# A channel-attention kernel: 160 rows packed in place of 144, 23 plain rows stored first, and a scale in two halves

## The chip, the cores and the metric

The kernel runs on one core of one Trainium2 chip. The metric is the device time of one execution in microseconds (us). The time before is 729.73 us, the median of three executions (729.52 to 731.41). A profile is one further execution, recorded by the hardware profiler; the profile before is of an execution of 729.56 us, whose instructions and transfers span 727.8 us.

The core's engines are named as in the profile: PE (TensorE: matmuls; PEld is its weight load), DVE (VectorE), ACT (ScalarE), POOL (GpSimd) and SP (SyncE). Loads from HBM are issued on SP's queue, stores on ACT's; both use the same 16 DMA engines.

## The reference

```python
H = W = C = 384;  r = 96                 # x: [1, 384, 384, 384] bf16, w1: [384, 96], w2: [96, 384]
xf  = x.reshape(B, H * W, C)
gap = jnp.mean(xf, 1)
gmp = jnp.amax(xf, 1)
h_a = relu(gap @ w1)
h_m = relu(gmp @ w1)
scale = sigmoid(h_a @ w2 + h_m @ w2)
return x * scale[:, None, None, :]
```

The whole of x (147,456 positions of 384 channels, 113.25 MB) has to be read before the first output can be computed, since the scale depends on the mean and the maximum over all positions. Then x is multiplied by one number per channel and written. What of x was kept on the chip after the first reading need not be read again.

## The kernel before

**Rows.** The positions are spread over the 128 partitions, 1152 on each. One position on all partitions is called a row here: 384 bf16 values on each partition, 98,304 bytes in all. A block of n rows is one transfer of n x 768 contiguous bytes for each partition.

**First pass.** All 1152 rows are loaded in the order of the list `loads`, by one DMA for each entry. Three large tiles, `slots` (44 rows each, `x` in the profile), are filled in turn; FILLS gives for each of 25 fills the rows that will be packed (always 16, `PAIR`) and the rows that are only looked at. For every load PE adds the rows up by matmuls with ones (`sums`, L274: three matmuls for up to four rows), and DVE takes the maximum into the 11 rows of `acc` (`larger`, L311). Consecutive maxima go alternately into two parts of `acc` (PARTS). Towards the end `acc` is folded from 11 rows to 6 and from 6 to 3 (FOLDS: how many loads before the end, and to what width), after which the parts are smaller.

**What stays on the chip.** Of the 1152 rows, 337 are kept on the chip between the passes: 132 that the three slots hold at the end of the first pass (`stay_b`, STAYING gives the pieces in which they are loaded), 35 in the plain rows of the tile `room` (`room_b`, ROOM_PIECES), 10 in `late`, 16 in PSUM (`kept_ps`) and 144 in packed form. The other 815 are read a second time: the 11 rows with which `acc` began, between the passes (`refill`), and 804 in the second pass (AGAIN: 18 blocks of 44 and one of 12).

**Packing.** Sixteen rows at a time, two groups of 8 (PACKED). ACT copies the high bytes apart (L321), takes signs (L324), copies the low bytes into the room (L339), PE mixes the high bytes with weights (L334, 18 matmuls in three groups of six), ACT writes the mixed code (L344) and tests that the code can be undone (L341 and L346, into the scratch tile `test`). 8 rows become 6 rows' worth of bytes (PLANE_ROWS) in `room`, whose layout is ROOM_ROWS plain rows and then the packed planes. While packing goes on, the plain rows are scratch space (`high`, `sign`, `test`, `diag`, flags); only after the last pack and after `judge` (L353 to L355, one number that says if all packs were good; if not, a branch at the end stores the packed rows again from x) can they be loaded.

**Between the passes.** `turn_sums` and `tail_sums` bring the sums of the last rows (SUM_TAIL: how many loads are summed by the second of them) and of all others into one column for each 128 channels, w1 and w2 are loaded, and the hidden layer of the mean is computed on PE and ACT. DVE folds `acc` to one row, PE transposes it (L418), DVE reduces (L419), PE multiplies by w1 (L422), DVE adds the hidden layers (L423), PE multiplies by w2 for all partitions (L424), ACT takes the sigmoid into `scale_bc` (L425).

**Second pass.** `order` lists the tiles that hold rows, in the order in which they are multiplied and stored. `put` multiplies a piece in place on DVE (L430) and issues its store on ACT's queue (L446). The order before is slot 0, slot 1, the room (ROOM_TURN = 2), slot 2, and then the blocks of AGAIN in the slots. FIRST_STORES and FIRST_READS give the pieces of the first tiles. The 11 rows of `acc` are stored after three pieces (ACC_STORES_AT). After LEAD tiles the loads of the next blocks into the free slots are issued on SP; each waits until the store of what the slot held has landed. From the turn after UNPACK_FROM on, each turn unpacks one group of 8 rows into the room (`unpack`: ACT L464, DVE L467 and L470, and the multiplication L430). The groups' places in the room (`packed_place`) are 8 rows apart; a group may only be unpacked where no plane lies that is still needed. The first four groups are stored as soon as they are there (`early_b`), which frees their 32 rows for the last four groups; the rest goes out in three stores near the end (ROOM_STORES), behind them the late rows, the last block and the rows from PSUM.

SP, ACT and DVE run in the program's order (`manual_schedule` in the second pass), and a wait of one instruction holds up all that stand behind it on the same engine. PE's order is laid down at build time.

Of the kernel before, what the change touches and what calls it, by code (L numbers as in the profile page):

```python
# [8 lines left out]
ACT = mybir.ActivationFunctionType  # L9
ALU = mybir.AluOpType  # L10
# [15 lines left out]

PACKED = 8
GROUP = 4
N_PACK = 18
PAIR = 2 * PACKED  # L30
HIGH = 0x3800
HIGH_BITS = 0x8700
PLANE_ROWS = PACKED // 2 + PACKED // GROUP
# [7 lines left out]

ROOM_ROWS = 35
EARLY = 4
assert all(
    ROOM_ROWS + (PLANE_ROWS * k) >= (k + 1) * PACKED for k in range(N_PACK - EARLY)
) and ROOM_ROWS + PLANE_ROWS * (N_PACK - EARLY) >= EARLY * PACKED

ACC_ROWS = 11  # L50
PARTS = {11: ((0, 6), (6, 11)), 6: ((0, 3), (3, 6)), 3: ((0, 3),)}
LATE_ROWS = 10
# [2 lines left out]

PSUM_PIECES = (4, 12)
FILLS = (
    ((16,), ()), ((), (40,)), ((), (44,)), ((16,), (28,)), ((), (44,)), ((), (44,)),
    ((16,), (28,)), ((), (43,)), ((), (27,)), ((16,), (27,)), ((), (44,)), ((), (44,)),
    ((16,), (28,)), ((), (36,)), ((), (40,)), ((16,), (20,)), ((), (36,)), ((), (32,)),  # L60
    ((16,), (28,)), ((), (27,)), ((), (28,)), ((16,), (24,)), ((), (23, 21)), ((), (20,)),
    ((16,), (12, 16)),
)
ROOM_PIECES = (8, 6, 5, 6, 5, 5)
STAYING = ((16, 14, 14), (11, 11, 11, 6, 5), (4, 4, 3, 3, 6, 6, 3, 3, 6, 3, 3))
ROOM_LOADS = 2
LATE_AT = (1, 3)
LATE_PIECES = (10,)

FOLDS = {9: 6, 1: 3}  # L70

AGAIN = (44,) * 18 + (12,)
FIRST_STORES = ((4, 4, 4, 7, 8, 8, 9), (10, 11, 11, 12), (16, 19))
FIRST_READS = ((10, 11, 11, 12), (44,))
LEAD = 2
ROOM_TURN = 2
ACC_STORES_AT = 3
ACC_STORES = ((6, 11), (0, 6))
UNPACK_FROM = 4
ROOM_STORES = (44, 36, 32)  # L80
SUM_TAIL = 3
MM_ROWS = 4


# [1 line left out]
def kernel(  # L86
# [7 lines left out]
    nc = tc.nc  # L94
    P = nc.NUM_PARTITIONS
    B_, H, W, C = x.shape
    R = w1.shape[1]
# [27 lines left out]
    early_b = block_of(EARLY * PACKED)  # L125
    packed_b = block_of(n_packed - EARLY * PACKED)
    late_b = block_of(LATE_ROWS)
    room_b = block_of(ROOM_ROWS)
# [10 lines left out]
    hid = small[0:R, 8:9]  # L139
# [14 lines left out]
    scale_bc = consts.tile([P, C], BF16)  # L154
    w2_sb = scale_bc[0:R, :]
# [11 lines left out]
    n_grp = PACKED // GROUP  # L167
# [15 lines left out]
    acc = hole[:, 0:A, :]  # L183
    late = hole[:, A:A + LATE_ROWS, :]

    scratch = PAIR + 2 * n_grp + PAIR // 2
    high = room[:, 0:PAIR, :]
    sign = room[:, PAIR:PAIR + 2 * n_grp, :]
    test = room[:, PAIR + 2 * n_grp:scratch, :]
    diag = room[:, scratch:scratch + 2, :].rearrange("p n c -> p (n c)").rearrange("p (k m) -> p k m", m=P)  # L190
    flags_bf = room[:, scratch + 2, 0:N_PACK // 2]
    scrap = room[FLAG:FLAG + 1, scratch + 2, N_PACK:N_PACK + N_PACK // 2]
# [20 lines left out]

    def packed_place(k):

        if k < EARLY:
            return early_b, k * PACKED
        if k < N_PACK - EARLY:
            return packed_b, k * PACKED
        return packed_b, (k - N_PACK + EARLY) * PACKED  # L220


    first = (-1 - len(FILLS)) % NS
# [5 lines left out]
    done, k = A, 0  # L229
# [15 lines left out]
    def pieces_of(block, pieces, buf):  # L245
        j = 0
        for m in pieces:
            loads.append((block, j, j + m, buf, j, ()))
            j += m
        assert j == block[1]  # L250

    for s, pieces in enumerate(STAYING):
        if s == ROOM_LOADS:
            pieces_of(room_b, ROOM_PIECES, room)
        n = len(loads)
        pieces_of(stay_b[s], pieces, slots[s])
        if s == LATE_AT[0]:
            j = 0
            for i, m in enumerate(LATE_PIECES):
                loads.insert(n + LATE_AT[1] + i, (late_b, j, j + m, late, j, ()))  # L260
                j += m
            assert j == LATE_ROWS
    n_loads = len(loads)
    judged_at = max(i for i, load in enumerate(loads) if load[5]) + 2
    tail_rows = sum(hi - lo for _, lo, hi, *_ in loads[n_loads - SUM_TAIL:])
# [100 lines left out]
    for i, (block, lo, hi, buf, at, groups) in enumerate(loads):  # L366
# [24 lines left out]
        j = 0  # L391
# [29 lines left out]
    for q in range(CQ):  # L421
        nc.tensor.matmul(hTm_ps, lhsT=w1_sb[:, q, :], rhs=gT[:, q, 1:2], start=(q == 0), stop=(q == CQ - 1))  # L422
    nc.vector.scalar_tensor_tensor(out=hid, in0=hTm_ps, scalar=0.0, in1=hid_a, op0=ALU.max, op1=ALU.add)  # L423
    nc.tensor.matmul(z_ps, lhsT=hid.to_broadcast([R, P]), rhs=w2_sb, start=True, stop=True)  # L424
    nc.scalar.activation(out=scale_bc, in_=z_ps, func=ACT.Sigmoid)  # L425


    def multiply(dst, src):
        n = dst.shape[1]
        nc.vector.tensor_tensor(  # L430
            out=dst, in0=src, in1=scale_bc.unsqueeze(1).to_broadcast([P, n, C]), op=ALU.mult
        )

    def put_acc():
# [4 lines left out]
    def put(block, buf, pieces, acc_at=None):  # L439
        j = 0  # L440
        for i, m in enumerate(pieces):
            if i == acc_at:
                put_acc()
            rows = buf[:, j:j + m, :]
            multiply(rows, rows)
            nc.scalar.dma_start(out=part(orr, block, j, j + m), in_=rows)  # L446
            j += m
        assert j == block[1]
# [7 lines left out]

    def unpack(k):
        low, code = planes(k)
        j = packed_place(k)[1]
        rows = room[:, j:j + PACKED, :]  # L460
        words = rows.bitcast(U16)
        bits = acc[:, 0:PACKED, :].bitcast(U16)
        more = acc[:, PACKED:PACKED + n_grp, :].bitcast(U16)
        nc.scalar.activation(out=words, in_=low, func=ACT.Copy, bias=float(HIGH))  # L464

        def field(out, shift, op, mask):
            nc.vector.tensor_scalar(out=out, in0=code, scalar1=shift, scalar2=mask, op0=op, op1=ALU.bitwise_and)  # L467

        def add(out, a, b):
            nc.vector.tensor_tensor(out=out, in0=a, in1=b, op=ALU.bitwise_or)  # L470

        for r in range(GROUP - 1):
            field(bits[:, r * n_grp:(r + 1) * n_grp, :], 4 * r, ALU.logical_shift_left, HIGH_BITS)
        last = bits[:, PACKED - n_grp:PACKED, :]
        field(more, 12, ALU.logical_shift_left, 0x8000)
        field(last, 4, ALU.logical_shift_right, 0x0700)
        add(last, last, more)
        add(words, words, bits)
        multiply(rows, rows)
# [10 lines left out]
        get(block, slots[s], reads.pop(0) if reads else (block[1],))  # L490
        order.append((block, s))

    room_left, j = [], EARLY * PACKED
    for m in ROOM_STORES:
        room_left.append((j, j + m))
        j = (j + m) % packed_b[1]
    assert j == EARLY * PACKED

    def put_room(count):
        for _ in range(count):  # L500
# [7 lines left out]
    while k < len(order):  # L508
        block, s = order[k]
        buf = room if s is None else slots[s]  # L510
        put(block, buf, stores.pop(0) if stores else (block[1],), None if k else ACC_STORES_AT)
        k += 1
        if k == LEAD:
            for j in range(k):
                read_into(order[j][1])
        elif k > LEAD:
            read_into(s)
        if k > UNPACK_FROM and unpacked < N_PACK:
            unpack(unpacked)
            unpacked += 1  # L520
            if unpacked == EARLY:
                nc.scalar.dma_start(out=part(orr, early_b, 0, early_b[1]), in_=room[:, 0:early_b[1], :])
        if k == n_turns - 2:
            put_room(1)
        elif k == n_turns - 1:
            put_room(2)
            multiply(late, late)
            nc.scalar.dma_start(out=part(orr, late_b, 0, LATE_ROWS), in_=late)
# [48 lines left out]
```

## Time and profile before

| what | value |
|---|---|
| median of three executions | 729.73 us |
| the profiled execution: time, span | 729.56 us, 727.8 us |
| DVE busy | 556.4 us, 76% of the span |
| ACT busy | 250.3 us, 34% |
| PE busy | 156.4 us, 21% |
| SP's queue (loads): share of the 16 DMA engines | 62.6%, 193.52 MB |
| ACT's queue (stores) | 36.4%, 113.25 MB |

"Busy" is the time in which an engine executed an instruction. An instruction's release is inferred from semaphore events. The profile's page also cuts the span into 40 slices of 18.2 us and gives, for each, the busy tenths of each engine, the granted PE clock, the share of the DMA engines' time and the bytes moved. The same can be asked for any stretch of time; the columns are then the stretch, its length, the busy time and count of PE, PEld, DVE, ACT and POOL, the granted PE clock (1.00 is full), the DMA share (which can pass 1 a little) and GB/s. The chain of waits follows the work that ended last back to its start.

### The profile page before, as it was taken

The page shows a single profiled execution, that of the slowest core. Times are in us where ns is not written, and L with a number is a line of the kernel's source. Part 1 is how long each engine was busy: PE and PEld are TensorE (multiplying, and loading weights), DVE is VectorE, ACT ScalarE, POOL GpSimd, SP SyncE. Part 2 cuts the span into 40 slices and gives each one's busy share as a digit, 9 for nine tenths or more (in the row PEclk, how much of TensorE's full clock was granted, in tenths as well). Part 3 has the DMA queues.
Part 4 walks back from the last instruction along what each step waited for, and adds up shares of the span by engine and source line. Part 5 has one row for each costly group of instructions (what it writes and reads, how often), then busy time and mean ns, then how long its engine had stood idle before and what let it go on. Part 6 is the DMA issues. An engine that isn't in the chain of part 4 may idle for free.

```text
span 727.8 us, 3125 instructions
## 1 busy us (share of the span) xinstructions
PE 156.4 (21%) x1069; PEld 50.5 (7%) x1078; DVE 556.4 (76%) x422; ACT 250.3 (34%) x135; POOL 0.7 (0%) x6
## 2 busy tenths in 40 slices
PE   3656654555666460000000000000000000000000
PEld 1211211111121120000000000000000000000000
DVE  6689999999999998978177677277767766666920
ACT  4994985978998400002011111011111011111100
POOL 0000000000000000000000000000000000000000
PEclk9975788877876755555555555555555555555555
DMA  9999999999999989999999999999999999999997
GB/s 384 426 440 413 429 444 420 426 435 419 429 425 421 416 315 355 404 430 449 423 446 416 438 445 420 446 416 446 436 425 442 419 444 420 444 440 431 435 421 340
DMA packets 19248, 306.96 MB, mean 422 GB/s; under 512 B 2496, under 2 KB 2848, under 8 KB 7200
## 3 DMA queue, kind: packets, MB, share of 16 engines
q1 hardware_dynamic: 13328, 193.52, 62.6%
q10 hardware_dynamic: 5904, 113.25, 36.4%
q8 instruction: 8, 0.13, 0.1%
q14 instruction: 8, 0.07, 0.0%
HBM read 193.51 MB, written 113.25 MB: 421 GB/s over the span
## 4 chain that ended last, share of the span: by engine, by line
DMA 60%; DVE 18%; ACT 14%; issue 2%; PE 1%; SPq 0%; DVEq 0%; ACTq 0%
DMA x<-in_x_dram 39%; DMA out_dram<-x 21%; DVE x L430 12%; ACT room L321 6%; ACT room L339 5%; DVE hole L311 5%; ACT room L324 2%; DVE room L430 1%; PE bank_b L334 1%; DVE hole L430 1%; ACT room L344 1%; PE bank_a L274 1%; ACT room L464 0%; DVE room L470 0%; SPq L369 0%
## 5 line engine op out<-in xcount | busy, mean ns | idle before, releaser
L430 DVE TENSOR_TENSOR x<-x,scale_bc 128x16896 bf16<-128x16896 bf16 (+7 forms) x31 | 191.3, 6194 | 93.5 <-DMA x<-in_x_dram 92.4
L311 DVE TENSOR_TENSOR hole<-hole,x 128x1920 bf16<-128x1920 bf16 (+3 forms) x215 | 235.8, 1175 | 15.8 <-DMA x<-in_x_dram 14.3
L464 ACT ACTIVATE room<-room 128x3072 uint16<-128x3072 uint8 x18 | 49.7, 2763 | 358.8 <-DVE x L430 358.8
L274 PE MATMUL bank_a<-x,small 128*1 128x512 bf16 x816 | 95.2, 492 | 59.5 <-DMA x<-in_x_dram 59.0
L321 ACT CAST room<-x 128x3072 bf16<-128x3072 uint8 x18 | 48.7, 2750 | 43.7 <-DMA x<-in_x_dram 43.7
L334 PE MATMUL bank_b<-room 128*128 128x512 bf16 x153 | 52.0, 465 | 43.8 <-ACT room L324 20.7
L339 ACT COPY room<-x 128x3072 uint8<-128x3072 uint8 x18 | 49.3, 2737 | 0.0
L470 DVE TENSOR_TENSOR room<-room,hole 128x3072 uint16<-128x3072 uint16 x18 | 31.6, 1758 | 23.0 <-ACT room L464 23.0
L341 ACT ACTIVATE room<-room,w_sb 128x6144 uint8<-128x6144 bf16 x9 | 48.7, 5407 | 0.0
L274 PEld LDWEIGHTS <-small 128*1 128x1 bf16 x861 | 29.5, 96 | 142.3 <-issue 128.0
L430 DVE TENSOR_TENSOR room<-room,scale_bc 128x3072 bf16<-128x3072 bf16 (+2 forms) x20 | 38.9, 1947 | 0.6
L467 DVE TENSOR_SCALAR hole<-room 128x768 uint16<-128x768 uint16 x90 | 25.7, 354 | 0.0
L346 ACT ACTIVATE room<-room,w_sb 128x3072 bf16<-128x3072 uint16 x9 | 25.7, 2853 | 0.0
L334 PEld LDWEIGHTS <-room 128*128 128x128 bf16 x162 | 17.1, 109 | 78.0 <-issue 70.4
L344 ACT ACTIVATE room<-bank_b 128x512 uint16<-128x512 f32 x27 | 15.9, 590 | 0.8 <-PE bank_b L334 0.7
L324 ACT ACTIVATE room<-x 128x1536 bf16<-128x1536 bf16 x9 | 13.3, 1478 | 0.0
L470 DVE TENSOR_TENSOR hole<-hole 128x768 uint16<-128x768 uint16 x18 | 10.0, 558 | 0.6
L299 ACT COPY w_sb<-bank_a 65x128 f32<-65x128 f32 x2 | 0.5, 262 | 24.1 <-PE bank_a L274 23.6
L311 DVE TENSOR_TENSOR hole<-hole,room 128x2304 bf16<-128x2304 bf16 (+2 forms) x7 | 7.7, 1156 | 0.0
L379 DVE COPY kept_ps<-x 128x768 uint32<-128x768 uint32 (+1 forms) x2 | 3.5, 1762 | 4.2 <-DMA x<-in_x_dram 4.2
L274 PE MATMUL bank_a<-room,small 128*1 128x512 bf16 (+1 forms) x27 | 4.3, 538 | 4.4 <-DMA room<-in_x_dram 4.4
L311 DVE TENSOR_TENSOR hole<-hole 128x384 bf16<-128x384 bf16 (+4 forms) x6 | 4.9, 823 | 0.1
(46 smaller groups left out, 29.1 us busy)
## 6 DMA issues: line engine op xcount, KB each, us to landing
x<-in_x_dram SPq DMA_DIRECT2D x22, 4224.0 KB, 26.8
out_dram<-x ACTq DMA_DIRECT2D x19, 4224.0 KB, 24.0
x<-in_x_dram SPq DMA_DIRECT2D x11, 1536.0 KB, 13.5
x<-in_x_dram SPq DMA_DIRECT2D x5, 2688.0 KB, 17.6
x<-in_x_dram SPq DMA_DIRECT2D x3, 2592.0 KB, 17.6
x<-in_x_dram SPq DMA_DIRECT2D x2, 3840.0 KB, 18.8
x<-in_x_dram SPq DMA_DIRECT2D x2, 3456.0 KB, 18.6
out_dram<-room ACTq DMA_DIRECT2D x2, 3072.0 KB, 31.2
```

Of the source, the lines that this page charges most:

```text
L274: nc.tensor.matmul(sum_ps[q * QP:q * QP + 1, 0:g * P], lhsT=ones_bf[:, 0:1], rhs=rows[:, :, q * P:(q + 1) * P], start=(summed == 0), stop= ...
L311: nc.vector.tensor_tensor(out=out, in0=a, in1=b, op=ALU.max)
L321: nc.scalar.copy(out=lanes[:, h], in_=halves[:, h, :, :, 1].rearrange("p (w g) c -> p w (g c)", g=n_grp))
L324: nc.scalar.activation(out=sign.rearrange("p (h g) c -> p h g c", h=2), in_=rows.rearrange("p (h n) c -> p h n c", h=2)[:, :, PACKED - n_g ...
L334: nc.tensor.matmul(pack_ps, lhsT=diag[:, w, :], rhs=flat(src)[:, i * 512:(i + 1) * 512], start=(w == 0), stop=(w == len(WEIGHTS) - 1),)
L339: nc.scalar.copy(out=planes(k + i)[0], in_=halves[:, i, :, :, 0])
L341: nc.scalar.activation(out=flat(test).bitcast(U8), in_=flat(high), func=ACT.Abs, bias=middle, scale=1.0 / STEP)
L346: nc.scalar.activation(out=flat(test), in_=flat(test).bitcast(U16), func=ACT.Square, bias=good, accum_out=flags[:, k // 2:k // 2 + 1],)
L430: nc.vector.tensor_tensor(out=dst, in0=src, in1=scale_bc.unsqueeze(1).to_broadcast([P, n, C]), op=ALU.mult)
L464: nc.scalar.activation(out=words, in_=low, func=ACT.Copy, bias=float(HIGH))
L467: nc.vector.tensor_scalar(out=out, in0=code, scalar1=shift, scalar2=mask, op0=op, op1=ALU.bitwise_and)
L470: nc.vector.tensor_tensor(out=out, in0=a, in1=b, op=ALU.bitwise_or)
```

## The change

- **N_PACK 18 to 20**: 20 groups (160 rows) are packed, so packs of 16 rows come in 10 of the 25 fills (fills 0, 3, 5, 8, 10, 13, 16, 19, 21 and 24) in place of 9 (every third).
- **ROOM_ROWS 35 to 23**: the plain rows in the room are as many fewer as the two groups need. AGAIN has 18 blocks of 44 and one of 8 rows (800 in place of 804). The scratch `test` moves from the room to the tile of `late`, which is therefore loaded after the last pack.
- **Order of the last loads**: the three slots, then the room, with the late rows (6 and 4) after the first piece of the room. The last four loads are room pieces of 3 rows. FOLDS comes 13 loads before the end (9 before), SUM_TAIL is 4 (3 before).
- **Places**: groups 0 to 7 take the places 0 to 7; groups 8 to 11 take the places 0 to 3 again, once the early store of 32 rows is out; groups 12 to 19 follow at 8 to 15. Unpacking starts one turn earlier (UNPACK_FROM 3), and in turn 12 two groups are unpacked. The stores of the room are 44, 44 and 40 rows.
- **Order of the second pass**: the room first (pieces 4, 4, 4, then `acc`, then 5 and 6), slot 0 in 7, 8, 9, 10, 10, slot 1 in four of 11, slot 2 whole; the next reads are issued after three tiles (LEAD 3), slot 0 in four pieces of 11.
- **Scale**: the product with w2 and the sigmoid are computed for channels 0 to 191 and 192 to 383 apart, and the first piece of the room is multiplied half by half.

```diff
-N_PACK = 18
+N_PACK = 20
-ROOM_ROWS = 35
+ROOM_ROWS = 23
 EARLY = 4
+AGAIN_AT = 8
+def place(k):
+    if k < AGAIN_AT:
+        return k * PACKED
+    return (k - AGAIN_AT if k < AGAIN_AT + EARLY else k - EARLY) * PACKED
...
-ROOM_PIECES = (8, 6, 5, 6, 5, 5)
-STAYING = ((16, 14, 14), (11, 11, 11, 6, 5), (4, 4, 3, 3, 6, 6, 3, 3, 6, 3, 3))
-ROOM_LOADS = 2
-LATE_AT = (1, 3)
-LATE_PIECES = (10,)
-FOLDS = {9: 6, 1: 3}
-AGAIN = (44,) * 18 + (12,)
-FIRST_STORES = ((4, 4, 4, 7, 8, 8, 9), (10, 11, 11, 12), (16, 19))
-FIRST_READS = ((10, 11, 11, 12), (44,))
-LEAD = 2
-ROOM_TURN = 2
+STAYING = ((11, 11, 11, 11), (10, 9, 6, 8, 5, 6), (5, 5, 5, 4, 4, 3, 6, 6, 6))
+ROOM_PIECES = (3, 3, 5, 3, 3, 3, 3)
+LATE_AT = 20
+LATE_PIECES = (6, 4)
+FOLDS = {13: 6, 1: 3}
+AGAIN = (44,) * 18 + (8,)
+FIRST_STORES = ((4, 4, 4, 5, 6), (7, 8, 9, 10, 10), (11, 11, 11, 11))
+FIRST_READS = ((11, 11, 11, 11), (44,))
+LEAD = 3
+ROOM_TURN = 0
-UNPACK_FROM = 4
-ROOM_STORES = (44, 36, 32)
-SUM_TAIL = 3
+UNPACK_FROM = 3
+UNPACK_TWO = 12
+ROOM_STORES = (44, 44, 40)
+SUM_TAIL = 4
...
-    scratch = PAIR + 2 * n_grp + PAIR // 2
+    scratch = PAIR + 2 * n_grp
-    test = room[:, PAIR + 2 * n_grp:scratch, :]
+    test = late[:, 0:PAIR // 2, :]
...
-    nc.tensor.matmul(z_ps, lhsT=hid.to_broadcast([R, P]), rhs=w2_sb, start=True, stop=True)
-    nc.scalar.activation(out=scale_bc, in_=z_ps, func=ACT.Sigmoid)
+    halves = ((0, C // 2), (C // 2, C))
+    for lo, hi in halves:
+        nc.tensor.matmul(z_ps[:, lo:hi], lhsT=hid.to_broadcast([R, P]), rhs=w2_sb[:, lo:hi], start=True, stop=True)
+    for lo, hi in halves:
+        nc.scalar.activation(out=scale_bc[:, lo:hi], in_=z_ps[:, lo:hi], func=ACT.Sigmoid)
...
-            multiply(rows, rows)
+            for lo, hi in halves if block is room_b and j == 0 else ((0, C),):
+                multiply(rows, rows, lo, hi)
...
-        if k > UNPACK_FROM and unpacked < N_PACK:
+        for _ in range((k > UNPACK_FROM) + (k == UNPACK_TWO)):
+            if unpacked == N_PACK:
+                continue
             unpack(unpacked)
             unpacked += 1
```

## The prediction

> **What bounds the kernel now.** First the page's row of slices and its transfers. The DMA engines are busy in all slices, at some 420 to 440 GB/s, with one dip in slices 15 and 16 (255 to 291 us). So the time is bytes divided by rate, plus what the dip loses.
>
> ```profile
> DMA  9999999999999989999999999999999999999997
> GB/s 384 426 440 413 429 444 420 426 435 419 429 425 421 416 315 355 404 430 449 423 446 416 438 445 420 446 416 446 436 425 442 419 444 420 444 440 431 435 421 340
> HBM read 193.51 MB, written 113.25 MB: 421 GB/s over the span
> ```
>
> Second, stretches of the span around the dip (last column GB/s). Loading ends near 268 us; 268 to 278 us moves little; stores alone run at 412, the start of the second reading at 357, then 433. From 700 to 724 us no engine computes and stores still drain at 430: the end is set by transfers.
>
> ```profile
> 200.00:250.00 50.00, 30.00 (x194) 9.21 (x198) 49.80 (x47) 41.60 (x25) 0.00 (x0) 0.70 1.01 423
> 250.00:264.00 14.00, 7.40 (x54) 1.64 (x49) 13.93 (x14) 0.00 (x0) 0.00 (x0) 0.64 1.02 404
> 268.00:272.00 4.00, 3.08 (x46) 2.98 (x47) 3.93 (x7) 1.06 (x5) 0.00 (x0) 0.50 0.36 109
> 276.00:278.00 2.00, 0.00 (x0) 0.00 (x0) 1.76 (x3) 0.21 (x1) 0.00 (x0) 0.50 0.17 60
> 278.00:292.00 14.00, 0.00 (x0) 0.00 (x0) 14.00 (x10) 0.00 (x0) 0.00 (x0) 0.50 1.02 412
> 292.00:298.00 6.00, 0.00 (x0) 0.00 (x0) 6.00 (x4) 0.00 (x0) 0.00 (x0) 0.50 1.01 357
> 500.00:700.00 200.00, 0.00 (x0) 0.00 (x0) 143.68 (x93) 27.63 (x10) 0.00 (x0) 0.50 1.00 433
> 700.00:724.00 24.00, 0.00 (x0) 0.00 (x0) 0.00 (x0) 0.00 (x0) 0.00 (x0) 0.50 1.00 430
> ```
>
> Third, the chain of waits through the dip (start, length, what): DVE's maxima, a fold, the last maximum, w2 on PE, the sigmoid on ACT, the first multiplication.
>
> ```profile
> 262.47 1.17 DVE hole L311
> 263.67 0.70 DVE hole L311
> ...
> 271.14 0.77 DVE hole L311
> ...
> 271.94 0.77 DVE hole L311
> ...
> 275.13 0.51 PE bank_a L424
> ...
> 275.72 0.50 ACT scale_bc L425
> ...
> 276.24 0.84 DVE x L430
> ```
>
> Fourth, ACT's instructions of the last pack: it starts when its rows land (221.73) and frees the slot's rows after 12.6 us (231.56 + 2.74 - 221.73); the whole pack takes 21.7.
>
> ```profile
> 221.73 5.40 ACT L321 CAST room<-x 128x3072 bf16<-128x3072 uint8 x2 [2.26 <-DMA x<-in_x_dram]
> 231.56 2.74 ACT L339 COPY room<-x 128x3072 uint8<-128x3072 uint8 x1
> 243.22 0.20 ACT L346 ACTIVATION_READ_ACCUMULATOR room<-room,w_sb 128x1 f32 x1
> ```
>
> **Part 1, four rows fewer to read.** 804 rows become 800, the 1152 stored stay. One turn of the second pass reads 44 and stores 44 rows; its stores are issued at 501.10 and 521.09, so a row costs 19.99 / 88 = 0.227 us, and four give -0.91. From the first store's issue to the end, (727.8 - 277.23) / 1956 rows = 0.230 gives -0.92. They would be free only if the end hung on DVE; its last instruction ends at 696.1, 28 us before the transfers. Taken: -0.91.
>
> **Part 2, scale in halves.** From L424 (275.13) to the first store's issue (277.23) is 2.10 us. ACT takes 0.26 for 128 elements (L299) and 0.49 for 384, so 0.32 for 192; PE for 192 columns some 0.35 (0.51 for 384); DVE's multiplication of four rows 0.87 from start to start, of half of it 0.47. If ACT starts after the first product: first half scaled at 0.35 + 0.05 + 0.32, second 0.32 later; the two half multiplications end near 1.75, store 1.82, a gain of 0.28. If ACT waits for both products, 0.70 and then the same, a loss of 0.07. The best, with the products overlapped, is 0.40. Taken: -0.28.
>
> **Part 3, the end of the first pass.** The list has 68 loads in place of 64. From 250 to 264, about 12 small loads moved 5.66 MB in 14 us, which takes 13.4 at 423 GB/s: 0.05 us a load, so loading ends some 0.2 later. The Trainium skill (DMA: Bandwidth & Descriptors, Bandwidth) asks for transfers of 1 MiB or more and gives each a fixed 2.0 us; these loads of 0.3 MB show 0.05, and if that rule held for queued loads, the term would be an estimated +8.0. But DVE ends last: from the fold at 262.47 its maxima run back to back, 11 of 3 rows in 7.45 us (0.67 each), to the fold at 271.14. In the changed program the fold comes after row 1098 of 1152; before, that row's maximum starts at 257.11, so with 0.2 for the loads and 0.9 for four rows the fold starts near 258.3. Behind it stand 16 maxima of 3 rows, one of 2 (0.47) and one of 1 (0.27): 1.2 + 16 x 0.67 + 0.74 = 12.7, and the fold to 3 starts near 271.1, as before. Taken: 0. Bounds: -0.9, if the longer stretch lets DVE catch up with the loads (it cannot gain more than it lags), and +0.6, if loading ends late by as much again as the extra loads cost (0.2) and DVE's lag is added to it.
>
> **Part 4, the tenth pack.** Packs' rows land 88 to 128 rows apart; at 0.2306 us a row (row 43 at 13.06, row 843 at 197.53) that is 20.3 us three times, and ACT, with 21.7, is late by at most 1.6 and catches up in the next gap. Queued behind a late pack are SP's refill of that slot and all later loads. The least time from a slot's release to the moment the load ahead of the refill has landed was 6.5 us before (released at 187.44, row 827 landing near 193.9); now it is 7.2 (released at 217.1, row 959 near 224.3). Cover holds: 0. The last pack's rows land 28 rows later, near 228.0; its test ends at 249.7, judge near 250.5 (244.3 before). The late rows now wait for that test, and behind them on SP stand all room loads, w1 and w2; they stand 33 rows before the end of loading, near 262, so 10 us remain. Upper bound if the cover went: three times 1.6, +4.8.
>
> **Part 5, two more unpacks.** One takes DVE 6.85 us (500.98 to 507.83) with the wait for ACT; DVE idles 4.27 for each block. In turn 12 two stand together: the next block's store comes 2.6 late. A block's store takes 24.0 to land and the next is issued after 20.0, so 4 us are still queued, and reads (26.8 to land) run beside it: 0, upper bound +2.6. Group 8 writes where the early store reads; ACT would hold all later stores if it waited, but the store is issued five turns (100 us) earlier, and stores of its size took 31.2 to land: 0.
>
> **Part 6, the room first, reads later.** The first reads wait until 78 rows are stored, not 55: stores alone last 23 x 0.235 = 5.4 us longer (23 rows at 412 GB/s), and the stretch of stores alone at the end is that much shorter. DVE needs 25.6 us for the first 122 rows, its 44-row piece is stored near 310.5, and from 297 to there 22 + 22 stores and 44 reads are queued, 88 x 0.23 = 20 us: no gap. Taken 0; bounds: the slow start of reading (357 in place of 412 over 6 us, 0.8) disappears or doubles.
>
> **Sum.** -0.91 - 0.28 = -1.2 from the profiled 729.56: 728.4. The median of the runs shown is 0.17 above that execution, so 728.5. Bounds together: -0.91 - 0.40 - 0.9 - 0.8 = -3.0, and, without the two covers, -0.91 + 0.07 + 0.6 + 0.8 = +0.6.
>
> **Rivals.**
> *Same traffic, no gain.* The halves gain nothing and the slow loads take the rest: 729.7. For it, every gain is under 1 us; against, the end is transfers alone.
> *Faster.* Reading starts behind a store queue that is fuller, and its slow start goes, with some of DVE's lag: 728.5 - 0.8 - 0.5 = 727.2. For it, 292 to 298 is slow only there; against, the four reads are of the same size as before.
> *Slower: PE's sums.* PE stands in order behind judge, now near 250.5. Then 20 groups of four rows wait, and 17 more arrive before the turn of the sums, at 267.9 before. At 0.42 a group (244 to 246, clock 0.50, 12 matmuls in 1.66) that is 15.5, done at 266. At the dearest row, 0.66, it is 24.4: the sums come 7 late, less 1.1 until the transposes would wait, so +5.9: 734.3. It decides from 0.50 on (18.5 us).
>
> ```profile
> 205.40 2.65 PE bank_a L274 x12
> ...
> 244.00:246.00 2.00, 1.66 (x12) 0.50 (x14) 2.00 (x2) 0.28 (x2) 0.00 (x0) 0.50 0.99 414
> 248.00:250.00 2.00, 2.00 (x33) 0.79 (x27) 2.00 (x3) 0.00 (x0) 0.00 (x0) 1.00 1.06 429
> ```
>
> Against it, within 4 us of steady sums after judge the granted clock rose from 0.50 to 1.00 and 11 groups took 2 us. The Trainium skill (TensorE: Matmul & The Clock Gate, Part 1) says that about 3.4 us of steady work lift the clock; the trace agrees, and by that rule this rival falls.
> *Slower: loads that don't overlap.* Each of the four extra loads costs what the load of w1 takes from issue to landing (72 KB, 2.0 us): +8.0, 736.5. It is the Trainium skill's rule of part 3. Against it, the 0.05 there; it decides from 0.9 us a load on.
> *Slower: packs.* The cover of part 4 goes: 728.5 + 4.8 = 733.3. For it, ACT is full three times; against, 7.2 us against 6.5.
>
> **How the numbers follow.** 0.3% (2.2 us) is about what a measurement of this kernel tells from no change: 727.5 to 731.9. Chances: my sum 0.53 (own range 727.5 to 729.5), no gain 0.12, faster 0.19, PE's sums 0.08, packs 0.07, loads 0.01. Part of the faster case stays within 0.3%, and of the slower ones what is half covered; unnamed causes go to both sides: faster 0.22, same 0.60, slower 0.18. The range, 726.5 to 731.9, takes in the lower bounds and leaves out the slower rivals.
>
> **What would show it.** Read bytes 0.39 MB fewer; the first fold of DVE near 258.3 and the last near 271.1; the first store near 276.9; the slice of the dip unchanged; judge near 250.5 and the turn of the sums still near 268; no slice of the first pass under 410 GB/s. A turn of the sums after 269, an idle DMA stretch before 260, or a rate other than 433 after 304 us makes the prediction wrong.

## The result and the profile after

The changed kernel takes 732.26 us (median of 20 executions, 729.16 to 736.63); the kernel before, run beside it, 729.75 (20 executions, 729.48 to 731.54). The ratio is 1.0029, with a 95% interval of 1.0015 to 1.0043: the change costs about 2 us, where 1.2 were to be won. The executions also lie further apart than before: 4 of the 20 took 729.16 to 729.35, less than any of the kernel before, and the other 16 took 731.06 or more, while 14 of the 20 of the kernel before took 729.48 to 729.84. The profiled execution of the changed kernel took 732.87 us with a span of 731.1, so 3.3 more than the one before; the balance below is made between these two, and no execution near 729.2 of the changed kernel was profiled.

The page's row of slices and its transfers:

```profile
DMA  9999999999999989999999999999999999999996
GB/s 372 422 427 438 425 431 429 430 424 426 424 427 419 411 313 365 378 431 448 422 425 429 437 434 433 435 431 431 440 429 431 440 429 431 436 434 425 435 433 293
HBM read 193.12 MB, written 113.25 MB: 419 GB/s over the span
```

The bytes are 0.39 MB fewer, as the change says. The first pass shows no new stretch of idle transfers. What differs is the slice where the second reading starts (378 in place of 404) and the last slice (293 in place of 340). Some of the stretches that the prediction shows, and the ones behind them (the last column is GB/s, the one before it the DMA share):

```profile
250.00:264.00 14.00, 10.03 (x94) 3.37 (x94) 13.93 (x16) 1.37 (x5) 0.00 (x0) 0.74 1.03 407
278.00:292.00 14.00, 0.00 (x0) 0.00 (x0) 14.00 (x11) 0.00 (x0) 0.00 (x0) 0.50 0.97 391
292.00:298.00 6.00, 0.00 (x0) 0.00 (x0) 6.00 (x4) 0.00 (x0) 0.00 (x0) 0.50 1.03 427
298.00:304.00 6.00, 0.00 (x0) 0.00 (x0) 6.00 (x3) 0.00 (x0) 0.00 (x0) 0.50 1.02 345
304.00:310.00 6.00, 0.00 (x0) 0.00 (x0) 6.00 (x1) 0.00 (x0) 0.00 (x0) 0.50 1.00 369
370.00:380.00 10.00, 0.00 (x0) 0.00 (x0) 7.60 (x9) 2.76 (x1) 0.00 (x0) 0.50 1.00 406
500.00:700.00 200.00, 0.00 (x0) 0.00 (x0) 145.37 (x93) 27.63 (x10) 0.00 (x0) 0.50 1.00 433
724.00:726.00 2.00, 0.00 (x0) 0.00 (x0) 0.00 (x0) 0.00 (x0) 0.00 (x0) 0.50 0.66 280
726.00:728.00 2.00, 0.00 (x0) 0.00 (x0) 0.00 (x0) 0.00 (x0) 0.00 (x0) 0.50 0.07 31
```

Three things are to be seen. Reading now starts at 298.8, and from there 12 us are slow (345 and 369), at a DMA share of 1.00 to 1.02: the engines are not idle, their packets take longer. There is a second slow stretch at 370. And after 726 one sixteenth of the DMA engines' time is used, at 31 GB/s: one engine alone is still storing. In the kernel before, these stretches were not slow, and it ended otherwise:

```profile
298.00:304.00 6.00, 0.00 (x0) 0.00 (x0) 6.00 (x2) 0.00 (x0) 0.00 (x0) 0.50 1.01 423
304.00:310.00 6.00, 0.00 (x0) 0.00 (x0) 6.00 (x2) 0.00 (x0) 0.00 (x0) 0.50 1.03 435
370.00:380.00 10.00, 0.00 (x0) 0.00 (x0) 8.65 (x9) 2.76 (x1) 0.00 (x0) 0.50 1.00 433
722.00:724.00 2.00, 0.00 (x0) 0.00 (x0) 0.00 (x0) 0.00 (x0) 0.00 (x0) 0.50 0.96 412
724.00:726.00 2.00, 0.00 (x0) 0.00 (x0) 0.00 (x0) 0.00 (x0) 0.00 (x0) 0.50 0.08 31
726.00:728.00 2.00, 0.00 (x0) 0.00 (x0) 0.00 (x0) 0.00 (x0) 0.00 (x0) 0.50 0.01 4
```

The trace records when each of the 16 engines has landed its part of a transfer. Of the last store, the first engine's part lands at 724.49 before and 725.42 after, the last engine's at 725.63 and 728.76. The distance between the two, called the lag here, is 1.1 us before and 3.3 after, and in the changed kernel 2.3 of it lie between the last engine and the next to last. So the 3.3 us are:

| part | us |
|---|---|
| first store issued later (277.23, now 277.80) | +0.57 |
| from there to the first engine's end, 447.26 to 447.62: four rows fewer, -0.91 by the prediction's term, and the rest, +1.27, put down to slow stretches | +0.36 |
| lag of the last engine (1.14 to 3.34) | +2.20 |
| from the last landing to the end of the span | +0.17 |

Without the growth of the lag and the slow stretches, 732.87 - 2.20 - 1.27 = 729.4 would be left. That is about where the shortest executions lie (729.16 to 729.35), so these two parts look like something that happens in most executions of the changed kernel and not in all; since none of those was profiled, this is not shown.

The chain of waits through the dip (start, length, what), in the changed kernel:

```profile
271.75 0.77 DVE hole L313
...
272.60 0.77 DVE hole L313
...
275.80 0.51 PE bank_a L428 x2
...
276.38 0.34 ACT scale_bc L430
...
276.75 0.90 DVE room L435 x2
```

DVE's last maximum starts at 272.60 (271.94 before). ACT starts 0.58 after the start of the first product with w2, when both products are done.

And ACT's instructions of the last pack, with PE's sums behind it (start, busy time, engine, line, what, count, idle time before):

```profile
228.85 5.41 ACT L323 CAST room<-x 128x3072 bf16<-128x3072 uint8 x2 [1.58 <-DMA x<-in_x_dram]
251.29 0.17 ACT L357 ACTIVATE room<-bank_a 1x10 bf16<-1x10 f32 x1 [0.26 <-PE bank_a L356]
```
```profile
251.72 8.98 PE L276 MATMUL bank_a<-x,small 128*1 128x512 bf16 x84 [0.47 <-ACT room L357]
261.60 0.38 PE L276 MATMUL bank_a<-x,small 128*1 128x512 bf16 x3 [0.90 <-DMA x<-in_x_dram]
```

The last pack waits for its rows (1.58 us), not its rows for it. PE has worked off its 28 queued groups at 260.7 and then waits for loads.

### The profile page after: what moved, and what is told of

It reads as the page before. It is cut to its first block, busy times and chain, and to the rows that moved or that the text cites. A ratio compares the mean times of both kernels' runs of the same rounds, so it can differ in the third digit from the quotient of the medians.

```text
span 731.1 us, 3221 instructions
## 1 busy us (share of the span) xinstructions
PE 159.8 (22%) x1087; PEld 52.2 (7%) x1097; DVE 563.9 (77%) x442; ACT 277.4 (38%) x149; POOL 0.7 (0%) x6
## 4 chain that ended last, share of the span: by engine, by line
DMA 53%; DVE 24%; ACT 14%; issue 2%; PE 1%; SPq 1%; ACTq 0%; DVEq 0%
DMA x<-in_x_dram 37%; DMA out_dram<-x 15%; DVE x L435 13%; DVE hole L313 8%; ACT room L323 4%; ACT room L341 4%; ACT room L471 2%; DVE room L435 2%; DVE room L477 1%; ACT room L326 1%; DMA hole<-in_x_dram 1%; ACT hole L343 1%; PE bank_a L276 1%; DVE hole L435 1%; ACT room L346 0%
## 5 line engine op out<-in xcount | busy, mean ns | idle before, releaser
L435 DVE TENSOR_TENSOR x<-x,scale_bc 128x16896 bf16<-128x16896 bf16 (+5 forms) x29 | 190.1, 6582 | 81.7 <-DMA x<-in_x_dram 81.7
L313 DVE TENSOR_TENSOR hole<-hole,x 128x1920 bf16<-128x1920 bf16 (+5 forms) x214 | 237.8, 1188 | 16.0 <-DMA x<-in_x_dram 14.7
L471 ACT ACTIVATE room<-room 128x3072 uint16<-128x3072 uint8 x20 | 55.2, 2762 | 352.7 <-DVE x L435 317.9
L336 PE MATMUL bank_b<-room 128*128 128x512 bf16 x170 | 59.0, 473 | 52.9 <-ACT room L326 20.9
L323 ACT CAST room<-x 128x3072 bf16<-128x3072 uint8 x20 | 54.0, 2750 | 28.7 <-DMA x<-in_x_dram 28.7
L341 ACT COPY room<-x 128x3072 uint8<-128x3072 uint8 x20 | 54.8, 2740 | 0.0
L343 ACT ACTIVATE hole<-room,w_sb 128x6144 uint8<-128x6144 bf16 x10 | 54.1, 5408 | 0.0
L435 DVE TENSOR_TENSOR room<-room,scale_bc 128x3072 bf16<-128x3072 bf16 (+4 forms) x26 | 40.3, 1564 | 1.7 <-ACT scale_bc L430 1.0
L348 ACT ACTIVATE hole<-hole,w_sb 128x3072 bf16<-128x3072 uint16 x10 | 28.5, 2854 | 0.0
L313 DVE TENSOR_TENSOR hole<-hole,room 128x1152 bf16<-128x1152 bf16 (+1 forms) x8 | 5.4, 728 | 0.1
```

Source lines behind the costliest of these rows:

```text
L313: nc.vector.tensor_tensor(out=out, in0=a, in1=b, op=ALU.max)
L323: nc.scalar.copy(out=lanes[:, h], in_=halves[:, h, :, :, 1].rearrange("p (w g) c -> p w (g c)", g=n_grp))
L336: nc.tensor.matmul(pack_ps, lhsT=diag[:, w, :], rhs=flat(src)[:, i * 512:(i + 1) * 512], start=(w == 0), stop=(w == len(WEIGHTS) - 1),)
L341: nc.scalar.copy(out=planes(k + i)[0], in_=halves[:, i, :, :, 0])
L343: nc.scalar.activation(out=flat(test).bitcast(U8), in_=flat(high), func=ACT.Abs, bias=middle, scale=1.0 / STEP)
L348: nc.scalar.activation(out=flat(test), in_=flat(test).bitcast(U16), func=ACT.Square, bias=good, accum_out=flags[:, k // 2:k // 2 + 1],)
```

## The experiments

The theory after the result (the engine out of step): the time is not bytes by the mean rate but the end of the last of 16 engines, and an engine that is behind when reading joins the stores stays behind. The expectations call it theory O (order) at first and theory E (engine) later; their theory P (packing) puts the loss ahead of the first store. Against the theory stood: four small reads in place of others, the halves of the scale, the packing itself, and the order of the second pass by another mechanism. All runs are compared with the kernel before on the same chip. First their numbers together; the last three columns are of one profiled execution each: the issue of the first store, the time from there to the first engine's end, and the lag.

| kernel | median, us | before, us | ratio, 95% interval | first store | to first end | lag |
|---|---|---|---|---|---|---|
| before | 729.75 | | | 277.23 | 447.26 | 1.1 |
| after | 732.26 | 729.75 | 1.0029 (1.0015 to 1.0043) | 277.80 | 447.62 | 3.3 |
| after again | 732.39 | 729.79 | 1.0024 (1.0004 to 1.0044) | 277.58 | 448.03 | 4.6 |
| old order | 730.42 | 729.79 | 1.0005 (0.9994 to 1.0016) | 277.37 | 446.97 | 1.5 |
| new order alone | 730.87 | 729.79 | 1.0011 (1.0003 to 1.0020) | 277.09 | 448.17 | 2.5 |
| whole first read | 733.35 | 729.79 | 1.0038 (1.0024 to 1.0051) | 277.66 | 450.58 | 5.4 |
| one scale | 733.09 | 729.68 | 1.0043 (1.0026 to 1.0060) | 277.81 | 449.16 | 5.0 |
| packing alone | 730.33 | 729.68 | 1.0004 (0.9987 to 1.0021) | 277.74 | 447.30 | 2.6 |
| halves alone | 729.57 | 729.68 | 1.0008 (0.9998 to 1.0018) | 277.04 | 447.27 | 1.1 |
| drained read | 732.18 | 729.68 | 1.0034 (1.0021 to 1.0046) | 277.85 | 449.39 | 1.0 |
| fold late | 731.33 | 730.34 | 1.0021 (1.0007 to 1.0034) | 278.31 | 448.84 | 1.8 |
| fewer loads | 731.07 | 730.34 | 1.0006 (0.9989 to 1.0023) | 278.02 | 446.36 | 1.1 |
| old order, drained | 730.36 | 730.34 | 1.0001 (0.9991 to 1.0011) | 277.37 | 447.48 | 1.8 |

A profiled execution is not always a typical one: those of "fewer loads" (729.45), of "halves alone" (729.44) and of "old order, drained" (729.85) were the fastest of their kernels, those of "whole first read" and "one scale" the slowest of theirs (737.33 and 736.09). The medians decide on the time, the last columns on where it lies.

### The changed kernel again

> The changed kernel once more, for the spread of its times and a second profile. Theory O (order): the loss lies where the second reading starts; one of the 16 DMA engines falls behind there by about 3 us and stays behind, so the last landings of a store are spread over 3 us or more from about 305 us to the end, and times lie at 731 to 734 us with some near 729.3. Theory P (packing): the loss lies before the first store; the first store is issued at 277.8 us or later in every profile, and the rest runs as before.

Measured: 732.39, and in the profile the same slow stretches (332 and 384 GB/s from 298 to 310, 409 from 370 to 380), a lag of 4.6 and one engine alone for the last 3.3 us of the stores (726.90 to 730.19); a window of its end:

```profile
728.00:730.00 2.00, 0.00 (x0) 0.00 (x0) 0.00 (x0) 0.00 (x0) 0.00 (x0) 0.50 0.06 25
```

The span is 1.4 longer than in the first profile of the same program (732.5 and 731.1), the lag 1.2 longer. So the lag also makes most of the difference between these two executions of one kernel. Theory P had asked for a first store at 277.8 or later; it came at 277.58. Of these 12 executions too, 3 took 729.07 to 729.34 and the others 731.02 or more.

### The packing with the old order of the second pass

```diff
-FIRST_STORES = ((4, 4, 4, 5, 6), (7, 8, 9, 10, 10), (11, 11, 11, 11))
-FIRST_READS = ((11, 11, 11, 11), (44,))
-LEAD = 3
-ROOM_TURN = 0
-UNPACK_FROM = 3
-UNPACK_TWO = 12
+FIRST_STORES = ((4, 4, 4, 7, 8, 8, 9), (10, 11, 11, 12), (11, 12))
+FIRST_READS = ((10, 11, 11, 12), (44,))
+LEAD = 2
+ROOM_TURN = 2
+UNPACK_FROM = 4
+UNPACK_TWO = (12, 13)
...
-            for lo, hi in halves if block is room_b and j == 0 else ((0, C),):
+            for lo, hi in halves if block is stay_b[0] and j == 0 else ((0, C),):
...
-        for _ in range((k > UNPACK_FROM) + (k == UNPACK_TWO)):
+        for _ in range((k > UNPACK_FROM) + (k in UNPACK_TWO)):
```

> The changed kernel with the second pass in the order of before (slot 0, slot 1, room, slot 2; reads of 10, 11, 11, 12; two turns with two unpacks). Theory O: the loss goes, 728.8 to 729.3 us with little spread, ratio 0.998 to 0.999. Theory P: as the changed kernel, 731.5 to 733 us, ratio 1.002 to 1.004.

Measured: 730.42, 2.0 less than the changed kernel on the same chip, and not to be told from before. Its end is that of before (37 GB/s from 724 to 726, then nothing). On this chip alone the intervals of "after again" and "old order" overlap. But all five measurements of the packed kernel in the new order have intervals above 1 (after, after again, whole first read, one scale, drained read), and of the five in the old order four include 1 (old order, packing alone, fewer loads, old order drained; fold late, which has another first pass, does not). So in the packed kernel the order of the second pass costs about 2 us. Neither theory had this time: O asked for 728.8 to 729.3 with little spread, P for 731.5 to 733. Without the new order the packing wins nothing that shows in the median, though its fastest execution (728.43) is 1.0 under the fastest of before (729.42).

### The new order without the packing

```diff
-FIRST_STORES = ((4, 4, 4, 7, 8, 8, 9), (10, 11, 11, 12), (16, 19))
-FIRST_READS = ((10, 11, 11, 12), (44,))
-LEAD = 2
-ROOM_TURN = 2
+FIRST_STORES = ((4, 4, 4, 5, 6, 6, 6), (7, 8, 9, 10, 10), (11, 11, 11, 11))
+FIRST_READS = ((11, 11, 11, 11), (44,))
+LEAD = 3
+ROOM_TURN = 0
```

> The kernel before with the second pass in the new order (room of 35 rows first, slot 0 in 7, 8, 9, 10, 10, slot 1 in four of 11, reads of four times 11) and nothing else. Theory O: it has the loss, 731.5 to 733.5 us with a wide spread, ratio 1.002 to 1.005. Theory P: 729.5 to 730, ratio 0.999 to 1.001.

Measured: 730.87, slower than before by 0.1% (0.03 to 0.20), less than the changed kernel's loss, and between what the two theories asked for (731.5 to 733.5 and 729.5 to 730). The first store comes as early as before, so the delay of the first store belongs to the packing. Reading starts slowly here too (376 and 393 from 298 to 310), and the lag is 2.5. But this lag did not arise at the start of reading: the transfers issued from 325 to 363 us land on all engines within 0.6 us, and only from 466 on are the engines more than 1.0 apart. The two parts together cost more than this one alone.

### One whole first read

```diff
-FIRST_READS = ((11, 11, 11, 11), (44,))
+FIRST_READS = ((44,), (44,))
```

> The changed kernel with the first read of the second pass as one load of 44 rows in place of four of 11. If the four small reads make the engine fall behind (a part of theory O), the loss goes: 728.8 to 729.5 us, ratio 0.998 to 1.000. If it is the depth of the store queue at that time, it stays: 731.5 to 733.5, ratio 1.002 to 1.005. Theory P: 731.5 to 733.

Measured: 733.35, no gain. The start of reading is less slow (380 and 427 from 298 to 310), and yet the lag is 5.4. Four small reads are not the cause; a slow start and a lag are two things. In this profile and in that of "one scale" time is also lost long after the start of reading: from 500 to 700 us they move 427 and 429 GB/s, where the kernel before and the changed one move 433.

### The scale whole, and the halves alone

The changed kernel with the scale in one piece:

```diff
-    halves = ((0, C // 2), (C // 2, C))
+    halves = ((0, C),)
```

> The changed kernel with the scale in one piece again. The theory of the first runs, E: one of the 16 DMA engines is about 1 us out of step when the second reading starts, falls behind there, and the end is its end. By the prediction's term for the halves this is 0.3 us slower than the changed kernel; by the two profiles of it (2.05 us from the last small DVE step to the first store, 2.14 before) 0.1 slower, which can't be told: 731 to 734 us. If the halves are what puts the engine out of step: 729.0 to 730.0, and the engine's lag shrinks before 298 us.

The kernel before with the halves alone, for the first piece that it stores:

```diff
+    halves = ((0, C // 2), (C // 2, C))
+    for lo, hi in halves:
+        nc.tensor.matmul(z_ps[:, lo:hi], lhsT=hid.to_broadcast([R, P]), rhs=w2_sb[:, lo:hi], start=True, stop=True)
...
+            for lo, hi in halves if block is stay_b[0] and j == 0 else ((0, C),):
+                multiply(rows, rows, lo, hi)
```

> The kernel before with the scale in halves and nothing else. Prediction's term: -0.28 us; by the profiles since: -0.1. 729.4 to 729.8, ratio 0.9995 to 1.0000. If halves put an engine out of step: 730.5 to 732 with a spread.

And the packing alone, which is the kernel with the old order and the scale in one piece:

> The changed kernel with the old order of the second pass and with one scale: the packing alone. Theory E: fastest times near 728.5 to 729 (0.39 MB fewer), median 729 to 730.5 with a spread as the old order with halves had (728.4 to 732.2). If it was the halves that spread those times: 728.6 to 729.2 with little spread.

Measured: 733.09, 729.57 and 730.33; none is told from its partner. In the traces, the stretch from the product with w2 to the issue of the first store is 2.10 to 2.11 with one scale (before, new order alone, packing alone, one scale) and 2.01 with the halves. The halves win 0.1 us; the loss stays without them, and alone they cause none.

### Reading that starts with drained engines

```diff
-            for j in range(k):
+            for j in reversed(range(k)):
                 read_into(order[j][1])
```

The first reads now go to slot 1, whose stores land later; SP issues them at 308.7 in place of 298.8, when most stores have drained.

> The changed kernel with the first two reads of the second pass exchanged: slot 1 (stored last) is read before slot 0, so reading starts only when all stores issued until then have landed, near 306 us, and the engines have run dry. It costs up to 2 us of idle engines. Theory E: the engines start in step, the last engine's lag stays under 1.5 us to the end, and times come close together, 729.5 to 731.5. If the lag has nothing to do with the start of reading: as the changed kernel or up to 2 us slower, 732 to 735, with a lag of 3 us or more at the end.

Measured: 732.18, so the time that the theory asked for (729.5 to 731.5) was missed. The six executions lie within 731.75 to 732.70, where the changed kernel's 20 lie 7.5 apart. Windows of the start and of the end:

```profile
304.00:310.00 6.00, 0.00 (x0) 0.00 (x0) 6.00 (x1) 0.00 (x0) 0.00 (x0) 0.50 0.75 272
370.00:380.00 10.00, 0.00 (x0) 0.00 (x0) 8.51 (x9) 2.76 (x1) 0.00 (x0) 0.50 1.00 433
```
```profile
724.00:726.00 2.00, 0.00 (x0) 0.00 (x0) 0.00 (x0) 0.00 (x0) 0.00 (x0) 0.50 1.02 436
726.00:728.00 2.00, 0.00 (x0) 0.00 (x0) 0.00 (x0) 0.00 (x0) 0.00 (x0) 0.50 0.57 240
728.00:730.00 2.00, 0.00 (x0) 0.00 (x0) 0.00 (x0) 0.00 (x0) 0.00 (x0) 0.50 0.02 4
```

The gap is there (272, at a share of 0.75), and costs the first engine 1.8 us (449.39 in place of 447.62). There is no slow stretch at 370, as there was none in "whole first read" and "one scale" either (433), and all engines end together: the lag is 1.0. The time is the same, by an idle stretch in place of a lag. This is the strongest evidence for the theory: the same rows, the same stores and reads but for their order, and after a start without a deep store queue the engines stay in step. It is one profile, though, and the same program up to the reads had its engines nearer together here already: the last was 0.6 to 0.7 us behind the next for the stores issued from 287 to 293, where it was 0.9 in the changed kernel.

### The same in the old order

The same edit in the packed kernel with the old order.

> The packed kernel with the second pass in its old order, and the two first groups of reads issued in the other order (slot 1 before slot 0), so that reading starts some 12 us later, when more stores have drained. By the theory of the engine out of step, a start of reading with the engines in step keeps them in step: the last engine ends within 1.3 us of the first, and the executions lie close together (within 1.0 of each other), as with the changed order, where the same edit gave 731.75 to 732.70; the idle stretch costs about 2, less what the lag costs: 729.5 to 731. If the order of the reads does not matter here, the time is that of the run with the old order, 728.4 to 732.2, with its spread.

Measured: 730.36, between 729.85 and 732.24, with nine of eleven executions from 729.85 to 730.86. The time is in the range that the theory asked for, but the same as that of the old order without the edit (730.42). The lag is 1.8 where 1.3 was asked for, in the fastest execution of this kernel, and the executions lie 2.4 apart where 1.0 was asked for. So this is no confirmation: most executions lie closer together than in the old order without the edit (728.43 to 732.15), but the engines did fall out of step, at about 510 us.

### What makes the first store late

Two candidates in the packed kernel with the old order: the longer stretch of narrow maxima,

```diff
-FOLDS = {13: 6, 1: 3}
+FOLDS = {9: 6, 1: 3}
```

> The packed kernel with the second pass in its old order (ROOM_TURN 2, LEAD 2 and the rest as in the run with the old order), and acc folded to 6 rows 9 loads before the end as before, in place of 13. The change's first store is issued 0.57 later than before (277.80 against 277.23), and the end of the first pass is one candidate. If the longer stretch of narrow maxima is what makes it late (theory: DVE), about 21 rows more are taken in wide maxima, DVE's last maximum starts near 271.9 in place of 272.6 and the first store is issued near 276.9 (277.37 in the run with the old order); time about 0.4 under that run (730.0 where it is 730.4). If the end of the loads sets it (theory: loads, whose first and last engine finish at 268.45 and 270.94 in place of 268.08 and 270.14), the last maximum stays at 272.4 to 272.7 and the time within 0.2 of that run.

and the number of loads:

```diff
-STAYING = ((11, 11, 11, 11), (10, 9, 6, 8, 5, 6), (5, 5, 5, 4, 4, 3, 6, 6, 6))
+STAYING = ((16, 14, 14), (11, 11, 11, 11), (8, 8, 7, 3, 6, 6, 6))
```

> The packed kernel with the second pass in its old order, and the rows of the three slots loaded by 14 DMAs in place of 19 (16, 14, 14; 11, 11, 11, 11; 8, 8, 7, 3, 6, 6, 6); the last 13 loads, the folds and everything else as in the run with the old order. If each extra load costs what I put it at (0.05 to 0.1), loading ends 0.25 to 0.5 earlier (first engine near 268.1, last near 270.4), DVE has its rows earlier, and the first store comes by up to 0.5 earlier, near 277.0. If loading ends late because the packing itself holds up something (the tenth pack's rows, the room loads behind its test), the end of the loads stays at 268.4 to 268.5 and the first store at 277.4. Time 729.9 against 730.4.

Both missed, in the time too (731.33 for 730.0, and 731.07 for 729.9). The late fold made the first store later, 278.31 in place of 277.37. DVE waited for a load before it (0.54 us, the bracket) and had no time to catch up behind it:

```profile
259.78 4.31 DVE L313 TENSOR_TENSOR hole<-hole,x 128x1920 bf16<-128x1920 bf16 x6 [0.54 <-DMA x<-in_x_dram]
264.13 1.16 DVE L313 TENSOR_TENSOR hole<-hole 128x1920 bf16<-128x1920 bf16 x1
...
273.10 0.76 DVE L313 TENSOR_TENSOR hole<-hole,room 128x1152 bf16<-128x1152 bf16 x1
```

With five loads fewer, the loads do end earlier, the first engine at 267.95 in place of 268.37: 0.08 us a load. But the first store comes at 278.02, because DVE's fold starts at 259.21 in place of 258.56 in the old order. So DVE sets the end of the first pass, as the prediction had it, and as far as these two runs show, what counts is how far it has come when the fold begins; loads that end earlier did not help it. Why fewer and larger pieces leave it further behind was not tried.

The second of these runs shows the term of the rows undisturbed. Its start of reading is slow once, as before (359, then 421 and 429), its lag is 1.1, as before, and from the first store to the first engine's end it takes 446.36, against 447.26: 0.90 less for four rows.

## Why the prediction was wrong, by its own steps

**The sum** failed at its base. "Bytes divided by rate, plus what the dip loses" holds for 16 engines that end together, as in the profile of before, where they end within 1.1 us. It has no term for an engine that falls behind. That is +2.2 of the 3.3 us. The run with drained engines points to the start of reading as its source, and does not settle it. The windows of the kernel before from 724 on show one engine that ends after the others; the prediction used them only to 724, and had no term for it.

**Part 6, the room first and reads later**, was taken as 0 with a bound of 0.8 either way, and is the step where it failed. With 160 packed rows the order of the second pass is what separates 732.4 from 730.4, and with 144 rows 730.9 from 729.8. The slow start did not move unchanged: it grew by 0.9, a little more than the bound. Against 433 GB/s, 298 to 310 lose (88 + 64) x 6 / 433 = 2.1 us, where 292 to 304 lost (76 + 10) x 6 / 433 = 1.2. A second slow stretch follows at 370 (27 x 10 / 433 = 0.6), which no part had; from 310 to 320 some 0.25 comes back (449 against 438). Together they are the 1.27 of the balance. And the lag came on top. "No gap" was right, the share stays at 1.00 or above from 292 to 310; it was the wrong question. The prediction's own sign of being wrong, a rate other than 433 after 304 us, came: 369 from 304 to 310 and 406 from 370 to 380.

**Part 3, the end of the first pass**, was taken as 0 with +0.6 as its bound; the packed kernels' first stores are 0.14 to 0.62 late, and 0.79 and 1.08 late in the two runs that changed the pass itself. The loads end 0.37 (first engine) to 0.80 (last) later, where 0.2 were taken, and the first fold starts at 259.00, not 258.3. Behind it the count was right: 12.7 forecast, 12.75 measured to the fold at 271.75. The Trainium skill (DMA: Bandwidth & Descriptors, Anatomy of one DMA — SWDGE (gpsimd) path) gives a transfer that GpSimd issues a fixed cost of about 2.0 us; the prediction names the section Bandwidth for it, which has the 1 MiB alone. The traces do not show that cost for these loads, which SP queues one behind the other: five fewer end 0.42 earlier.

**Part 2, the halves**, was taken as -0.28 and is worth -0.10. ACT waits for both products, the case that I priced at a loss of 0.07, with 0.70 for the products one after the other. They overlap: the second starts 0.13 after the first, and both are done after 0.50, as the whole product was. The gain that is left comes from the first half multiplication, which starts 0.37 after the sigmoid's start, where it was 0.52.

**Part 1, four rows**, was right: -0.91 forecast, -0.90 from the first store on, where no further slow stretch covers it. In the medians the late first store and the lag cover it. Even an execution without the lag and the slow stretches would not have reached 728.5: parts 2 and 3 were to bring the first store 0.28 earlier, and it came 0.57 later.

**Part 4 and part 5** held. The last pack's rows landed at 228.85 (forecast 228.0) and judge was over at 251.7 (250.5); no slice of the first pass is under 410 GB/s but the first one (372, and 384 before); from 500 to 700 the rate is 433 in both kernels.

The prediction's 1.6 for how late a pack can be is 1.4 by its own figures (21.7 - 20.3), which changes nothing.

**The rivals.** PE's sums fell: the queued groups took 0.32 each, 28 in 8.98 us, and the turn of the sums on ACT began at 269.00. That is just at the mark of 269 which I had set for the prediction to be wrong, but for the loads' delay, not for PE, which waited for them. Packs and loads that don't overlap fell too. "Same traffic, no gain" describes the packing with the old order (730.42 against 729.79). The slower side came by a mechanism that I had not named: all three slower rivals lay in the first pass, and the loss is in the second.

## What stays open

In the profiles of the changed kernel, of its repetition, of "whole first read" and of "one scale", one engine is 0.9 to 1.0 us behind the next while the stores run alone (stores issued from 287 to 293); in the kernel before, that distance shrinks from 0.6 to 0.2. These four then have lags of 3.3 to 5.4. In the old order the packed kernels show distances of 0.2 to 1.1 up to the start of reading and lags of 1.1 to 2.6, and "new order alone" starts with 0.4 to 0.6 and still ends at 2.5. So being out of step at the start goes with the lag, but does not fix its size. What puts the one engine behind after the packed first pass was not found.

The landings of the transfers issued from 325 to 363 us, when reading has joined, say more. In the four profiles with the long lags the first and the last engine land a transfer 2.2 to 8.5 us apart there. In the kernel before they are 0.3 apart, stay within 0.5 until 564 and part only at 571 us, so its lag of 1.1 has nothing to do with the start of reading; in "new order alone" they are 0.6 apart, in "drained read" 0.8 to 2.1. In "fold late" they are 3.1 to 4.9 apart, and yet the lag at the end is 1.8. So the theory fits how the changed kernel loses its engine, but an engine that is behind does not always stay behind, and engines in step at 340 us can part later. The landings give times and no engine's number, so that it is the same engine throughout is inferred. What starts the later stretches was not tried. Nor was it shown, beyond the two profiles of the changed kernel, that the lag makes the spread between executions of one kernel, since only profiled executions record the landings.

No kernel tried here beats the one before: the best, the packing with the old order with or without drained engines, is not to be told from it.

## What to carry to other kernels

Where transfers set the end, look at the last few microseconds by engine: a DMA share of one sixteenth there is one engine that is behind, and saved bytes need not show while it is. When loads are made to join a deep queue of stores at another point, expect the joint itself to change price, and bound it by more than the stretch that is slow today. A saving of under 1 us in a kernel whose executions differ by 2 is decided by such effects, so price them before the bytes.

## What the runs showed of the hardware

- The median full packet of 33,792 bytes takes 1.251 us on its engine in every one of these profiles, 27.0 GB/s, and none takes less than 1.248. While one engine works alone at the end it is no faster (25 to 31 GB/s in the windows). So no trace here shows an engine that is behind running faster to catch up. In the kernel before the engines came together all the same, from 1.1 us apart at the first store to 0.3 at 341 us, and packets took longer in between. The Trainium skill (DMA: Bandwidth & Descriptors, Why a DMA increments its semaphore by 16 and not by 1) says that the 16 engines of a transfer finish independently; the traces agree, with 1.0 to 5.4 us between them at the last store.
- When reads join stores, packets take longer for 6 us (before) to 12 us (changed kernel) while the engines are busy throughout. Against the median packet of the same size, the excess from 290 to 310 is 1.1 us for each engine in the kernel before and 2.1 in the changed one; the worst packet takes 0.4 us more in the one and 1.5 in the other.
- The same program differs from execution to execution by up to 7.5 us (729.16 to 736.63) with the same instructions and bytes.
